# A recurrence feeding a mixture layer on one core: other numbers in the plan's model of transfers, three weight tiles in halves, and the first loads in halves under a limit of bytes in flight

## The chip, the cores and the metric

The kernel runs on one core of a Trainium2 chip. The metric is the device time of one execution in microseconds, as the median of several executions. The profile shows one execution in detail; its own time stands beside the median below.

## The reference

Two layers follow one another. The first is a linear recurrence for 4 batches and 8 heads with 48 dimensions and 768 steps; a state of 48 x 48 is decayed by a sigmoid of a gate, takes in the product of k and v, and is read by q. The second takes the 3072 tokens of 384 features through a layer with 2048 hidden features and the activation mish.

```python
f = 1.0 / (1.0 + np.exp(-f_logit))
for t in range(S):
    state = f[:, :, t, :, None] * state + np.einsum('bhd,bhe->bhde', k[:, :, t], v[:, :, t])
    y[:, :, t] = np.einsum('bhd,bhde->bhe', q[:, :, t], state)
...
h = x @ w_in
sp = np.where(h > 20.0, h, np.log1p(np.exp(np.minimum(h, 20.0))))
g = h * np.tanh(sp)
return (g @ w_out).astype(np.float32)
```

## The kernel before

**Work.** The recurrence is done in 24 chunks of 128 steps (6 blocks of time x 4 batches), numbered so that four chunks in a row, one of each batch, make a group of 512 tokens. A chunk's attention (`prep`, `attn0` to `attn3`) takes two loads of 0.524 MB, one with gates and k (`lk`) and one with q and v (`qv`); it ends with the attended columns in `xt`, or, for the first group, in `xs`. The second layer runs over 6 groups (g) and 16 tiles of 128 hidden features (j): nine products from `xt` into a bank `h` (`moe_in`, line 227), mish on ScalarE and VectorE (`mish`, lines 243 to 258), nine products into three banks `o` (`moe_out`, line 265). Values are split into a high and a low part, so that three products stand for one. For the first group the first four tiles (`WHOLE = 4`) are multiplied unsplit instead (`whole_in`, line 235, and `whole_out`, line 238).

**Weights.** Both weight matrices come as 64-bit data, 0.786 MB per tile j, into one of two `raw` buffers. `load_w` loads a tile and unpacks it with one operation of ScalarE and three of VectorE, of which line 371 is the last and frees the raw buffer; `split_w` makes the high and low part.

**Order.** Every step is added to a `Plan` with its engine, an estimated cost, the step that issues it, and what it reads and writes. The plan then packs all steps onto the engines, forwards and backwards in turn and under several settings, ranks them by how late each may run, and keeps the order whose modelled end is earliest. It issues the steps in that order, so the order on every engine, and on SP's queue for the loads, is fixed by the plan. In its model a load occupies SP for 500 ns, moves at 0.38 KB per ns behind the loads before it, and its readers may start 1550 ns after (`LATENCY["sp"]`, line 53, and lines 114 and 123). Where the plan sees TensorE idle before the first `whole_out` or `moe_out` step, it issues fillers (`idle`, line 353): products with zeros into a bank that is not in use.

**Halves.** The list `units` (line 652) gives the order of (g, j, columns) in the second layer. Tile 0 of the first group is worked in two halves of 256 columns (`EARLY_J = 1`), chunks 0 and 1 first, then 2 and 3; all others have 512 columns. A unit's products out come two units after its products in (`LAG = 2`). The units share two banks `h`, two buffers of mish and three of its result, by the unit's number. `EARLY = 24` says for which units mish squares on ScalarE and takes the low part on VectorE; later ones square on VectorE and take the low part on GpSimd. `attend_goal` says how many attention steps are added before each unit.

**Pacing.** `fetch` (line 342) issues a load on SP's queue. Loads 3 to 11 wait until the load three before them has landed (`AHEAD`, `PACED`); later ones wait only until their buffer is free.

Of the kernel before, what the change touches and what calls it, by code (L numbers as in the profile page):

```python
# [11 lines left out]
I32 = mybir.dt.int32  # L12
# [7 lines left out]
P = 128  # L20
C = 128
CH = C // 2
# [14 lines left out]
LAG = 2  # L37
L_CAP = -40.0
NTRI = GC
PACED = 12  # L40
AHEAD = 3
EARLY = 24
EARLY_J = 1
WHOLE = 4


class Plan:
# [2 lines left out]

    LATENCY = {"pe": 230.0, "act": 170.0, "dve": 160.0, "pool": 180.0, "sp": 1550.0}
    FREE = {"pe": 1500.0, "act": 1900.0, "dve": 1200.0, "pool": 2100.0, "sp": 600.0}

    def __init__(self):
# [3 lines left out]
    def add(self, engine, cost, issue, reads=(), writes=(), size=0, port=False):  # L60

        n = len(self.steps)
        before = {self.writer[r] for r in reads if r in self.writer}
        for w in writes:
            before |= set(self.readers.get(w, ()))
            before |= {self.writer[w]} if w in self.writer else set()
        for r in reads:
            self.readers.setdefault(r, []).append(n)
        for w in writes:
            self.writer[w], self.readers[w] = n, []  # L70
        before.discard(n)
        self.steps.append((engine, cost, issue, before, size, port or engine == "pool"))

    def pack(self, rank, ahead, haste, back=False):


        steps = self.steps
        count = len(steps)
        engine, cost, port = [s[0] for s in steps], [s[1] for s in steps], [s[5] for s in steps]
        before = [s[3] for s in steps]  # L80
        after = [[] for _ in steps]
        for i in range(count):
            for b in before[i]:
                after[b].append(i)
        if back:
            before, after = after, before
        free = dict.fromkeys(self.FREE, 0.0) if back else dict(self.FREE)
        queue = {e: [] for e in free}
        left, ready, start = [len(b) for b in before], [0.0] * count, [0.0] * count
        for i in range(count):  # L90
            if not left[i]:
                queue[engine[i]].append(i)
        transfers = shared = 0.0
        for _ in range(count):
            best = None
            for e, q in queue.items():
                if q:
                    at = [(max(ready[i], shared) if port[i] else ready[i], i) for i in q]
                    t0 = max(free[e], min(at)[0])
                    _, t, i = min(  # L100
                        (rank[i] + haste * max(0.0, r - t0), max(free[e], r), i)
                        for r, i in at if r <= t0 + ahead
                    )
                    if best is None or t < best[0]:
                        best = t, i
            t, i = best
            e = engine[i]
            queue[e].remove(i)
            start[i] = t
            end = free[e] = t + cost[i]  # L110
            if port[i]:
                shared = end
            if e == "sp" and not back:
                transfers = max(transfers, end + 650.0) + steps[i][4] / 0.38
                end = transfers - 650.0
            for a in after[i]:
                f = a if back else i
                if engine[i] == engine[a] == "pe":
                    lag = 0.0
                else:  # L120
                    lag = self.LATENCY[engine[f]]
                    if back and engine[f] == "sp":
                        lag += steps[f][4] / 0.38
                ready[a] = max(ready[a], end + lag)
                left[a] -= 1
                if not left[a]:
                    queue[engine[a]].append(a)
        return start
# [36 lines left out]
def T_ACT(n, psum=False, bias=0):  # L165
    return n / 1.2 + (50 if psum else 92) + 93 * bias + 2


def T_DVE(n):
    return n / 0.96 + 70  # L170
# [7 lines left out]
def recurrence_moe_kernel(  # L178
# [12 lines left out]
    nc = tc.nc  # L191
# [76 lines left out]
    with tc.tile_pool(name="work", bufs=1) as pool, tc.tile_pool(  # L268
# [28 lines left out]
        def inputs(n):  # L297

            whole, place = (held[n], n) if n in held else (in_[n % 2], n % 2)
            keys = [pairs((x, place)) for x in "lkq"] + [[("v", place)]]  # L300
            return keys, [whole[:, x].rearrange("p (a c) -> p a c", a=NP) for x in range(3)] + [whole[:, 3]], whole

        plan = Plan()
        add = plan.add
# [34 lines left out]

        issued = []  # L340

        def fetch(dst, src):

            ins = nc.sync.dma_start(dst, src)
            if AHEAD <= len(issued) < PACED:
                tc.add_manual_dep(
                    ins.ins, issued[-AHEAD].ins.name,
                    mybir.DependencyInfo(mybir.DependencyClass.Sync, mybir.DependencyReason.SCHED_ONLY), reason="pace",
                )
            issued.append(ins)  # L350

        def idle():
            nc.tensor.matmul(zeros[:, 0:P], state0[:, 0:P], state0[:, 0:P], start=True, stop=True)
# [2 lines left out]
        def load_w(j):  # L356

            raw, t = raw_[j % 2], wt_[j % 2]  # L360
            low, high = raw[:, :, 0], raw[:, :, 1]
            kr, kt = ("raw", j % 2), ("wt", j % 2)
            whole, kw = (first[j].bitcast(I32), ("first", j)) if j < HF else (t, kt)
            add("sp", 500, lambda: fetch(raw.rearrange("p a b -> p (a b)"), ww[j].bitcast(I32)),
                (), [kr], 786)
            add("act", T_ACT(W_TILE), lambda: nc.scalar.activation(
                t.bitcast(F32), high.bitcast(F32), AF.Copy, scale=2.0**-112), [kr], [kt])
            add("dve", 480, lambda: nc.vector.tensor_scalar(t, t, 3, None, ALU.logical_shift_left), (), [kt], port=True)
            add("dve", T_DVE(W_TILE), lambda: nc.vector.scalar_tensor_tensor(  # L369
                t, low, 29, t, ALU.logical_shift_right, ALU.bitwise_or), [kr], [kt], port=True)  # L370
            add("dve", T_DVE(W_TILE), lambda: nc.vector.scalar_tensor_tensor(
                whole, high, -(2**31), t, ALU.bitwise_and, ALU.bitwise_or), [kr, kt], [kw], port=True)

        def split_w(j):
            w, kw = (first[j], ("first", j)) if j < HF else (wt_[j % 2].bitcast(F32), ("wt", j % 2))
            old = [[], []]
            if j >= HF:
                old = [
                    [k for n in held for x in inputs(n)[0] for k in x]
                    + [("s", ("xt", 0, c), t) for c in range(GC) for t in range(NP)],  # L380
                    [("first", i) for i in range(HF)],
                ]
            add("act", T_ACT(W_TILE), lambda: nc.scalar.activation(weights(j)[0], w, AF.Copy), [kw], [("w", "h", j)] + old[0])
            add("dve", T_DVE(W_TILE), lambda: nc.vector.tensor_tensor(
                weights(j)[1], w, weights(j)[0].bitcast(F32), ALU.subtract), [kw, ("w", "h", j)],
                [("w", "l", j)] + old[1], port=True)
# [10 lines left out]
        def load(n):  # L397
            keys, _, whole = inputs(n)
            for x, src in ((0, lk), (2, qv)):
                add("sp", 500, lambda x=x, src=src: fetch(whole[:, x : x + 2], src[n]),  # L400
                    (), keys[x] + keys[x + 1], 524)

        def prep(n, parts):
# [237 lines left out]
        steps = [(f, n) for n in range(GC + 1) for f in (start, attn1, attn2, attn3)][:-1]  # L641
# [9 lines left out]

        units = [(0, j, x) for x in range(2) for j in range(EARLY_J)] + [(0, j, 2) for j in range(EARLY_J, HF)]
        units += [(1, j, 2) for j in range(HF)] + [(g, j, 2) for g in range(2) for j in range(HF, NF)]
# [3 lines left out]
        def attend_goal(u):  # L657

            per = 4 * GC
            u = u // 2 if u < 2 * EARLY_J else u - EARLY_J  # L660
            if u < NF + HF:
# [61 lines left out]
        for u in range(len(units) + LAG):  # L723
            if u < len(units):
                g, j, part = units[u]
                whole = g == 0 and j < WHOLE
                if g == 0 and part != 1:
                    load_w(j)
                    if not whole:
                        split_w(j)  # L730
                if u == EARLY_J + WHOLE:
                    split_x()
                if g == 1 and j < WHOLE:
                    split_w(j)
                x, hs, us, gs = g % 2, u % 2, u % 2, u % 3
# [32 lines left out]
    with tc.If(good < total):  # L768
# [3 lines left out]
        with tc.tile_pool(name="slow", bufs=1) as pool, tc.tile_pool(  # L772
# [9 lines left out]
            with tc.For_i(0, B, 1) as b:  # L782
                with tc.For_i(0, NP, 1) as p:
                    f, k, q = (st([P, NCB, C], nm) for nm in ("sf", "sk", "sq"))
# [34 lines left out]
            with tc.For_i(0, NG, 1) as g:  # L819
                x = st([P, NK, GT], "sx")  # L820
                tok = ds(g * GT, GT)
                rows = xs.rearrange("(a e r m) t -> a e m r t", e=2, r=D // 3, m=3)
                with tc.For_i(0, NK, 1) as a:
                    for e in range(2):
                        for m in range(4):
                            src = rows[ds(a, 1), e, m, :, tok] if m < 3 else rows[NP - 1, e, ds(a, 1), :, tok]
# [7 lines left out]
                n, g_ = (st([P, GT], nm) for nm in ("sn", "sg"))  # L834
# [89 lines left out]
```

## Time and profile before

| What | Value |
|---|---|
| Median of 3 runs | 511.36 us (509.66 to 512.45) |
| Profiled execution: its own time | 512.86 us |
| Profiled execution: span from first to last instruction | 511.1 us |
| TensorE busy | 492.9 us, 96% |
| ScalarE busy | 357.9 us, 70% |
| VectorE busy | 340.6 us, 67% |
| GpSimd busy | 143.8 us, 28% |
| Mean granted TensorE clock | 0.99 |
| Loads and stores on SP's queue | 47.59 MB |

The shares are means over the whole span; the fillers count as TensorE's work in them. The work before about 60 us (loads, the first chunks, the first weights) differs from the long steady part behind it, so the rows below are taken by stretch. An idle time "<-issue" is one for which the profile shows nothing that was waited for.

### The profile page before, as it was taken

The numbers are of one execution on the slowest core, as the hardware profiler recorded it, in microseconds if no ns is written. First come the engines' busy times: TensorE is split into PE (matmuls) and PEld (weight loads), VectorE is DVE, ScalarE is ACT, GpSimd is POOL, SyncE is SP. The second block draws the span as 40 slices with busy tenths as digits, with TensorE's granted clock in tenths as the row PEclk, the third lists the DMA queues.
The fourth block names the chain that finished last, engine by engine and source line by source line (L and its number), as shares of the span: only waits on it lengthen the run. The fifth ranks groups of instructions, "written<-read, shape, count | busy, mean of one in ns | idle before, by whom it ended". The sixth has DMA issues, their size and how long they took to land.

```text
span 511.1 us, 12735 instructions
## 1 busy us (share of the span) xinstructions
PE 492.9 (96%) x5320; PEld 391.9 (77%) x5320; DVE 340.6 (67%) x584; ACT 357.9 (70%) x675; POOL 143.8 (28%) x126
## 2 busy tenths in 40 slices
PE   7789999989999999999999999999999999999994
PEld 7676567868788777787888788788788878888883
DVE  4598999989955775877577676586676454534441
ACT  6488998889986676676676676676686655655560
POOL 0331111100002343253343344244252223332421
PEclk9799999999999999999999999999999999999998
DMA  8855664444300542511121221121130000010001
GB/s 283 294 170 206 206 201 166 166 146 162 113 12 0 165 140 105 179 49 42 58 100 42 107 81 42 42 94 63 58 122 9 3 3 31 22 41 1 0 0 68
DMA packets 14800, 48.45 MB, mean 95 GB/s; under 512 B 1744, under 2 KB 1744, under 8 KB 14736
## 3 DMA queue, kind: packets, MB, share of 16 engines
q1 hardware_dynamic: 14736, 47.59, 26.8%
q8 instruction: 42, 0.69, 0.5%
q14 instruction: 22, 0.18, 0.1%
HBM read 39.32 MB, written 6.29 MB: 89 GB/s over the span
## 4 chain that ended last, share of the span: by engine, by line
PE 82%; DMA 6%; DVE 5%; ACT 2%; issue 2%; SPq 0%; DVEq 0%; ACTq 0%
PE o L265 35%; PE h L227 34%; DMA raw<-ww 3%; DMA in<-lk 2%; PE at L564 2%; PE at L552 2%; PE at L509 2%; PE at L468 2%; PE o L238 1%; PE at L576 1%; DMA spareh<-lk 1%; DMA in<-qv 1%; PE h L235 1%; DVE inv L430 1%; DVE wt L369 1%
## 5 line engine op out<-in xcount | busy, mean ns | idle before, releaser
L227 PE MATMUL h<-xt,wh 128*128 128x512 f32 x552 | 173.4, 395 | 2.3 <-DVE ng L256 1.6
L248 POOL TENSOR_TENSOR gl<-ng,gh 128x512 fp32r<-128x512 f32 x73 | 101.7, 1395 | 246.8 <-ACT gh L258 166.8
L227 PEld LDWEIGHTS h<-xt,wh 128*128 128x128 f32 x552 | 102.4, 188 | 26.7 <-DVE ng L256 3.7
L265 PE MATMUL o<-gh,wh 128*128 128x512 f32 x276 | 111.0, 402 | 0.0
L265 PE MATMUL o<-gl,wh 128*128 128x512 f32 x276 | 108.1, 392 | 0.0
L227 PE MATMUL h<-xt,wl 128*128 128x512 f32 x276 | 108.0, 391 | 0.0
L265 PE MATMUL o<-gh,wl 128*128 128x512 f32 x276 | 107.7, 390 | 0.0
L254 ACT ACTIVATE ng<-ng,half 128x512 f32<-128x512 f32 (+1 forms) x97 | 69.6, 717 | 48.5 <-DVE ng L244 46.5
L256 DVE SCALAR_TENSOR_TENSOR ng<-ng,h 128x512 f32<-128x512 f32 x92 | 63.1, 685 | 55.3 <-ACT ng L255 54.3
L252 DVE TENSOR_SCALAR ng<-ng 128x512 f32<-128x512 f32 (+1 forms) x97 | 47.7, 492 | 64.2 <-ACT ng L251 63.8
L251 ACT ACTIVATE ng<-h 128x512 f32<-128x512 f32 (+1 forms) x97 | 57.1, 589 | 43.8 <-PE h L227 43.3
L258 ACT ACTIVATE gh<-ng 128x512 fp32r<-128x512 f32 x92 | 57.5, 625 | 14.3 <-DVE ng L256 10.9
L255 ACT ACTIVATE ng<-ng 128x512 f32<-128x512 f32 (+1 forms) x97 | 60.4, 622 | 1.5
L265 PEld LDWEIGHTS o<-gh,wh 128*128 128x128 f32 x276 | 51.8, 188 | 12.0
L227 PEld LDWEIGHTS h<-xt,wl 128*128 128x128 f32 x276 | 51.8, 188 | 11.9
L265 PEld LDWEIGHTS o<-gl,wh 128*128 128x128 f32 x276 | 51.8, 188 | 11.8
L265 PEld LDWEIGHTS o<-gh,wl 128*128 128x128 f32 x276 | 51.9, 188 | 10.5
L244 DVE TENSOR_TENSOR ng<-ng 128x512 f32<-128x512 f32 x73 | 53.7, 736 | 2.2
L310 POOL TENSOR_TENSOR in<-in,inv 128x512 f32<-128x512 f32 x20 | 24.3, 1217 | 71.1 <-ACT inv L436 46.4
L430 DVE TENSOR_TENSOR_SCAN inv<-gate,state 128x516 f32<-128x516 f32 x20 | 24.9, 1243 | 1.6 <-ACT gate L421 1.4
L598 POOL TENSOR_TENSOR state<-tmp,ends 128x192 f32<-128x192 f32 x20 | 13.7, 682 | 26.1 <-PE at L552 15.7
L624 DVE TENSOR_TENSOR xt<-at,xt 128x256 fp32r<-128x256 f32 x40 | 15.8, 419 | 7.3 <-ACT xt L623 6.9
(135 smaller groups left out, 528.8 us busy)
## 6 DMA issues: line engine op xcount, KB each, us to landing
raw<-ww SPq DMA_DIRECT2D x16, 768.0 KB, 4.2
in<-lk SPq DMA_DIRECT2D x22, 512.0 KB, 3.8
in<-qv SPq DMA_DIRECT2D x22, 512.0 KB, 3.6
out<-ob SPq DMA_DIRECT2D x18, 256.0 KB, 2.3
xt<-xt SPq DMA_DIRECT2D x15, 128.0 KB, 2.5
half<-ob SPq DMA_DIRECT2D x6, 256.0 KB, 2.3
ob<-half SPq DMA_DIRECT2D x6, 256.0 KB, 3.2
spareh<-lk SPq DMA_DIRECT2D x2, 512.0 KB, 5.2
```

Source lines behind the costliest of these rows:

```text
L227: nc.tensor.matmul(h, w[:, a * P : (a + 1) * P], xt[:, x, a, cols], start=(n == 0), stop=(n == 3 * NK - 1))
L244: ("dve", T_DVE(w), 1, lambda: nc.vector.tensor_tensor(n, n, n, ALU.mult))
L248: ("pool", T_POOL(w), 1, lambda: nc.gpsimd.tensor_tensor(gl, g, gh.bitcast(F32), ALU.subtract))
L251: ("act", T_ACT(w, True), 0, lambda: nc.scalar.activation(n, h, AF.Exp)),
L252: ("dve", T_DVE(w / 2), 1, lambda: nc.vector.tensor_scalar(n, n, E_CAP, 1.0, ALU.min, ALU.add)),
L254: ("act", T_ACT(w, False, 1), 0, lambda: nc.scalar.activation(g, n, AF.Ln, bias=half1, scale=0.5)),
L255: ("act", T_ACT(w), 0, lambda: nc.scalar.activation(g, g, AF.Exp, scale=-1.0)),
L256: ("dve", T_DVE(w), 0, lambda: nc.vector.scalar_tensor_tensor(gw if whole else g, g, 1.0, h, ALU.subtract, ALU.mult)),
L258: ("act", T_ACT(w), 0, lambda: nc.scalar.activation(gh, g, AF.Copy)),
L265: nc.tensor.matmul(o, w, x, start=(first and i == 0), stop=(last and i == 2))
L310: add("pool" if on_pool else "dve", cost, lambda: eng.tensor_tensor(dst, x, y, ALU.mult), reads, writes, port=port)
L430: add("dve", 2 * T_DVE(w + st) - 70, lambda s=s, st=st: nc.vector.tensor_tensor_scan(inv1[:, s].rearrange("p a c -> p (a c)"), gate[:, s]. ...
```

## The change

Three things change together. The model of transfers in the plan gets a rate of 0.32 in place of 0.38 KB per ns and a delay of 2400 in place of 1550 ns. `EARLY_J` goes from 1 to 3, so tiles 0, 1 and 2 of the first group are worked in halves of 256 columns: the three first halves, then the three second halves. And each of the first 16 loads is issued as two transfers, of rows 0 to 63 and of rows 64 to 127; each of the 32 waits for the latest earlier one without which at most 1100 KB, itself included, are in flight.

```diff
-PACED = 12
-AHEAD = 3
+PACED = 16
+FLIGHT = 1100
 EARLY = 24
-EARLY_J = 1
+EARLY_J = 3
...
-    LATENCY = {"pe": 230.0, "act": 170.0, "dve": 160.0, "pool": 180.0, "sp": 1550.0}
+    LATENCY = {"pe": 230.0, "act": 170.0, "dve": 160.0, "pool": 180.0, "sp": 2400.0}
...
-                transfers = max(transfers, end + 650.0) + steps[i][4] / 0.38
+                transfers = max(transfers, end + 650.0) + steps[i][4] / 0.32
...
-                        lag += steps[f][4] / 0.38
+                        lag += steps[f][4] / 0.32
...
-        def fetch(dst, src):
-
-            ins = nc.sync.dma_start(dst, src)
-            if AHEAD <= len(issued) < PACED:
-                tc.add_manual_dep(
-                    ins.ins, issued[-AHEAD].ins.name,
-                    mybir.DependencyInfo(mybir.DependencyClass.Sync, mybir.DependencyReason.SCHED_ONLY), reason="pace",
-                )
-            issued.append(ins)
+        def fetch(dst, src, size):
+
+            early = len(issued) < 2 * PACED
+            for r in (slice(0, CH), slice(CH, P)) if early else (slice(0, P),):
+                ins = nc.sync.dma_start(dst[r], src[r])
+                if early:
+                    issued.append((ins, size / 2))
+                    flight, n = 0, len(issued)
+                    while n and flight + issued[n - 1][1] <= FLIGHT:
+                        n -= 1
+                        flight += issued[n][1]
+                    if n:
+                        tc.add_manual_dep(
+                            ins.ins, issued[n - 1][0].ins.name,
+                            mybir.DependencyInfo(mybir.DependencyClass.Sync, mybir.DependencyReason.SCHED_ONLY), reason="pace",
+                        )
```

The two callers of `fetch` pass the size of the load, 786 for weights and 524 for a chunk.

## Rows read from the trace of the kernel before

**Rows 1.** Stretches: length, busy PE, PEld, DVE, ACT, POOL; clock, DMA share, GB/s.

```profile
6.50:16.00 9.50, 9.10 (x202) 7.76 (x203) 4.32 (x11) 8.65 (x23) 2.29 (x2) 1.00 0.93 319
16.00:19.40 3.40, 0.03 (x3) 0.00 (x0) 1.02 (x2) 0.98 (x2) 0.71 (x2) 0.99 0.93 351
19.40:26.20 6.80, 6.79 (x96) 6.03 (x99) 5.10 (x8) 2.46 (x6) 1.58 (x2) 0.50 0.74 242
26.20:41.00 14.80, 12.99 (x401) 11.02 (x393) 13.91 (x21) 13.08 (x33) 4.36 (x4) 1.00 0.48 171
41.00:57.50 16.50, 15.37 (x194) 8.97 (x190) 14.93 (x30) 14.71 (x31) 2.87 (x3) 1.00 0.63 211
57.50:110.00 52.50, 50.23 (x700) 36.85 (x700) 49.88 (x83) 45.60 (x87) 7.22 (x7) 1.00 0.54 184
...
135.00:160.00 25.00, 25.00 (x110) 20.13 (x109) 16.66 (x28) 20.76 (x36) 1.13 (x1) 1.00 0.13 43
160.00:504.50 344.50, 344.17 (x3514) 276.78 (x3512) 207.80 (x357) 224.47 (x417) 122.53 (x98) 1.00 0.17 59
```

**Rows 2.** The waits of TensorE, 0 to 40 us: total, times, longest.

```profile
PE h L468 <- issue: 3.4, 1, 3.4
```

**Rows 3.** Groups by form, 26.2 to 41 us: total busy us, mean ns.

```profile
L353 PE MATMUL o<-state 128*128 128x128 f32 x16 | 2.4, 281 | 0.0
```

**Rows 4.** Timeline of SP's queue: start us, duration us, issue.

```profile
0.75 0.39 SPq L344 DMA_DIRECT2D in<-lk  x1
...
4.47 1.53 SPq L344 DMA_DIRECT2D spareh<-lk  x2
...
16.72 0.33 SPq L344 DMA_DIRECT2D in<-lk  x1
19.28 0.33 SPq L344 DMA_DIRECT2D in<-qv  x1
```

**Rows 5.** The chain of waits, 40 to 110 us: start us, us, what.

```profile
42.64 6.13 DMA raw<-ww
...
99.31 6.66 DMA raw<-ww
```

**Rows 6.** The waits of ScalarE, 0 to 140 us.

```profile
ACT wt L366 <- DMA raw<-ww: 4.0, 3, 2.0
```

**Rows 7.** The waits of TensorE, 40 to 130 us.

```profile
PE h L227 <- DVE ng L256: 1.6, 1, 1.6
```

**Rows 8.** Timeline of VectorE: the unpacking of weight tiles 1 and 2 ends.

```profile
28.78 0.94 DVE L371 SCALAR_TENSOR_TENSOR sparel<-raw,wt 128x768 int32<-128x768 int32 x1
...
36.62 1.71 DVE L371 SCALAR_TENSOR_TENSOR sparel<-raw,wt 128x768 int32<-128x768 int32 x1
```

**Rows 9.** Timeline of TensorE, 20 to 54 us.

```profile
21.28 1.13 PE L468 MATMUL o<-spareh 48*64 48x64 f32 x32
...
31.91 1.46 PE L235 MATMUL h<-spareh,sparel 128*128 128x256 f32 x6
...
40.98 1.56 PE L235 MATMUL h<-spareh,sparel 128*128 128x256 f32 x6
...
52.75 1.56 PE L238 MATMUL o<-ob,sparel 128*128 128x256 f32 x6
```

**Rows 10.** Groups by form, 30 to 60 us: mish at 512 and 256 columns.

```profile
L251 ACT ACTIVATE ng<-h 128x512 f32<-128x512 f32 x3 | 1.8, 587 | 0.0
...
L254 ACT ACTIVATE ng<-ng,half 128x512 f32<-128x512 f32 x2 | 1.4, 722 | 0.0
...
L254 ACT ACTIVATE ng<-ng,half 128x256 f32<-128x256 f32 x2 | 1.0, 506 | 0.0
...
L251 ACT ACTIVATE ng<-h 128x256 f32<-128x256 f32 x2 | 0.8, 384 | 0.0
```

**Rows 11.** The page: costliest groups; DMA issues, us to landing.

```profile
L244 DVE TENSOR_TENSOR ng<-ng 128x512 f32<-128x512 f32 x73 | 53.7, 736 | 2.2
...
raw<-ww SPq DMA_DIRECT2D x16, 768.0 KB, 4.2
```

More of the change, by code (lines that the diff above doesn't have):

```diff
@@ L363, in load_w @@
             whole, kw = (first[j].bitcast(I32), ("first", j)) if j < HF else (t, kt)
-            add("sp", 500, lambda: fetch(raw.rearrange("p a b -> p (a b)"), ww[j].bitcast(I32)),
+            add("sp", 500, lambda: fetch(raw.rearrange("p a b -> p (a b)"), ww[j].bitcast(I32), 786),
                 (), [kr], 786)
@@ L399, in load @@
             for x, src in ((0, lk), (2, qv)):
-                add("sp", 500, lambda x=x, src=src: fetch(whole[:, x : x + 2], src[n]),
+                add("sp", 500, lambda x=x, src=src: fetch(whole[:, x : x + 2], src[n], 524),
                     (), keys[x] + keys[x + 1], 524)
```

## The prediction

> **What bounds the kernel now.** I read four views in this order. First the stages, as busy time in stretches [rows 1]. From 57.5 us on TensorE is full: 50.23 of 52.50 us up to 110 us, 25.00 of 25.00 between 135 and 160, 344.17 of 344.50 up to 504.5 us. Only 2.27 us are lost in the first of these and 0.33 in the last. So whatever the change brings must come out of the first 57.5 us, or out of those 2.27. VectorE and ScalarE stand beside it at 49.88 and 45.60 of 52.50 us between 57.5 and 110 us, and VectorE falls to 16.66 of 25 us after 135 us: early on the engines that unpack weights are nearly full too.
>
> Second, where the early time of TensorE goes. The profile calls an engine busy that runs the fillers of line 353 (products with zeros, into a bank that nobody reads yet), so the busy column flatters. [...] Between 26.2 and 41.0 us TensorE is busy 12.99 of 14.80 us [rows 1], and 2.4 us of that is fillers [rows 3]: 1.8 + 2.4 = 4.2 us without useful work. From 41.0 to 57.5 us 1.13 us are idle [rows 1].
>
> Third, the transfers. SP issues the early loads in order; the third-latest must have landed before the next is issued. Read so, the issue at 4.47 us is the landing of the first load (0.524 MB), and that at 19.28 us the landing of the ninth, the second weight tile [rows 4]. By then seven loads of 0.524 MB and two of 0.786 MB have landed, 5.24 MB, so the stream runs at (5.24 - 0.52) / (19.28 - 4.47) = 0.319 MB per us. The first load took 4.47 - 0.75 = 3.7 us. The old plan believed 0.38 and 0.50 + 1.38 + 1.55 = 3.4 us; the new one 0.32 and 0.50 + 1.64 + 2.40 = 4.5 us. For the rate the new number is what the trace shows. At 0.38 the 5.24 MB are over 2.6 us earlier than at 0.32, so the old plan placed consumers too early.
>
> Fourth, what that error costs behind 41 us: the chain of waits has the raw weight loads of 42.64 and 99.31 us, 6.13 and 6.66 us long [rows 5], where the old model gives 0.50 + 2.07 + 1.55 = 4.1 us and the new one 0.50 + 2.46 + 2.40 = 5.4. ScalarE stood 4.0 us in front of raw weights in the first 140 us [rows 6]. TensorE felt it as 1.6 us in front of a product after mish [rows 7].
>
> **The change part by part.** All sums are made against the profiled execution, 512.86 us (a span of 511.1 us). The median of the runs shown is 511.36 us, 1.5 us below, and I subtract the same gap from it.
>
> **Three tiles in halves (EARLY_J, line 43; units, line 652).** The first product of a tile can start when chunks 0 and 1 have been attended, not all four. Before, only tile 0 did. Now tiles 1 and 2 may too. Tile 1's unpacking ends at 28.78 + 0.94 = 29.7 us [rows 8]; its half can lie in the 4.2 us hole between 26 and 41 us. A half costs 1.46 us in and 1.56 us out [rows 9], 3.0 us. I credit 2.5 us: bounds are 0 (it only displaces other work) and 4.2 (the whole hole). Tile 2 is unpacked at 36.62 + 1.71 = 38.3 us [rows 8], too late for the hole; its half gains nothing. It may even cost: the units share two h banks, two mish buffers and the o banks in the order of the list, and tile 2's first half now stands ahead of the second halves of 0 and 1. Tile 0's second half ran at 40.98 us [rows 9], 2.7 us after 38.3, so as long as tile 2 is no more than some 2 us later than before nothing waits for it. The price: two tiles run mish twice at 256 columns. Two of ScalarE's four operations show the extra, 2 x 0.384 - 0.587 = 0.18 us and 2 x 0.506 - 0.722 = 0.29 us [rows 10]; eight operations at 0.235 make 1.9 us of ScalarE, which is 14.71 of 16.50 us busy between 41.0 and 57.5 us [rows 1], so some 0.8 us will show (bounds 0 and 1.9). Two late tiles of group 0 also change form, because EARLY counts units: their subtraction goes to GpSimd and their square to VectorE, which has 8.3 of 25 us free there [rows 1]. That costs nothing under this cover, and 2 x 0.736 = 1.5 us without it [rows 11].
>
> **The plan's model (lines 53, 114 and 123).** Consumers of a load are placed later and loads earlier, on all queues. The gain is bounded by TensorE's waits that go back to a late load: 1.13 us between 41.0 and 57.5 us and 1.6 of the 2.27 behind, 2.8 us in all [rows 1, 7]; below by 0, or by a loss of the same size if the new order puts something else late. For a raw tile on its own the new model is too slow (median 4.2 us to landing against its 5.4) [rows 11], so some consumers stand later than they need. I take 2.2 us. More delay in the plan also means more fillers before the first product; they lie in front of the first data and cost nothing.
>
> **Halves of 64 rows and 1.1 MB in flight (line 342 on).** The first 16 loads become 32 issues. SP pays an issue of 0.33 us [rows 4] for 16 more, 5.3 us on a queue that waits for landings most of that time; each consumer waits for two landings in place of one. In flight were three loads, 1.57 MB or more; now four halves of 0.262 MB, or two of 0.393 with one of 0.262. A load of 0.524 MB took 3.7 us, of which 1.6 us at 0.32 is the moving, so 2.1 us is delay; a window of 1.05 MB turns over in 2.1 + 0.8 = 2.9 us, 0.36 MB per us, just above the rate of the stream. Two weight halves alone, 0.786 MB in 3.3 us, give 0.24, so a weight tile beside another costs up to 0.9 us. I take 0.6 us for bubbles (bounds 0 and, with a lower rate, rival 2). Nothing lands earlier by it, since the loads were already in order.
>
> **Sum:** -2.5 - 2.2 + 0.8 + 0.6 = -3.3 us: 509.5 us for the profiled execution, **508.0 us** for the median. Its own range, from the bounds of the two credits, is 505 to 511 us.
>
> **Rivals.** (1) *The gain is taken by the unpacking.* TensorE gets ahead, but between 57.5 and 110 us VectorE has only 52.50 - 49.88 = 2.6 us free [rows 1], and TensorE, 3 us earlier, waits there for mish and weights. For it: those digits. Against it: part of VectorE's work there unpacks weights used long after. That gives 510.8 us (509.5 to 514).
>
> (2) *Slower: the halves move at a lower rate.* Each transfer now writes 64 neighbouring rows, and all in flight sit on SP's one queue, one behind another. No row shows such a transfer; a load of 128 rows is the nearest, at 0.319 MB per us. If halves run at two thirds, 0.21, the ninth load (5.24 MB) lands at some 2 + 25 = 27 us instead of 19.3, and tile 1 is unpacked 8 us later, at the end of the hole: the 2.5 us are gone. The eighth load, q and v of chunk 2 (4.46 MB, landed when the issue of 16.72 us goes out [rows 4]), lands at 23 us, and TensorE, which took its scores at 21.28 us [rows 9], would stand some 4 us later, 2.5 us of which the hole behind takes back. Net 4 - 2.5 + 0.8 + 0.6 = +2.9 us on the median, 514.3 us (511.5 to 518). It decides below about 4.46 / (21.3 - 2 - 3) = 0.27 MB per us, with 3 us from landing to the scores; above that nothing on the path is late. [...]
>
> (3) *Faster: the stall at 16 us and the slow clock go.* The 3.4 us are no wait for data that the trace shows, and the new plan has other fillers and another order in front of that place. If the stall falls on a gap, 3.4 us and half of the 6.8 us at 0.50 [rows 1, 2] are saved, less what the chunk loads would hold up then: some -4.5 us more than the forecast, 503.5 us (500 to 506). As easily it stays or falls elsewhere.
>
> **How the numbers follow.** Forecast 0.42, rival 1 0.20, rival 2 0.26, rival 3 0.12. A difference under 0.5% (2.6 us: under 508.8 is faster, over 513.9 slower) is about what a measurement can't tell from none. Of the forecast 0.30 lies under 508.8 and 0.12 between; of rival 1 0.18 between and 0.02 above; of rival 2 0.05 between and 0.21 above; rival 3 is faster. Faster 0.42, same 0.35, slower 0.23. The range for 8 in 10 leaves out most of rival 3 below and the upper part of rival 2: 502.5 to 516.5 us.
>
> **What would show it.** Right: products of line 235 at 256 columns for three tiles, tile 1's first before 41 us, and fewer fillers after 26 us; TensorE full from about 54 us; raw weights no longer waited for by ScalarE. Rival 1: new waits of TensorE for mish or the low part of weights between 55 and 110 us. Rival 2: well under the 319 GB/s of before between 6.5 and 16 us [rows 1], with the DMA share still high. Rival 3: no stretch at 0.50. The prediction is wrong if TensorE's useful work at 57.5 us is not ahead of before by about 3 us.

## The result, and the profile after

| Kernel | Median of 4 runs | Against before, 95% interval | Profiled execution |
|---|---|---|---|
| before | 511.14 us | 1 | 512.86 us |
| changed | 516.42 us | 1.0107 (1.0069 to 1.0146) | 515.46 us |

The changed kernel is slower by 1.1%, 5.3 us of the medians. The forecast was 508.0 us and faster; the time is inside the range, close to its upper end, on the side of rival 2. The profiled executions differ by only 2.6 us: the one of after is its fastest, the one of before is slower than each of the runs that make its median.

The stretches of the changed kernel, with the columns of [rows 1]: length, busy time of the engines, granted clock, DMA share, GB/s.

```profile
core 0: us, PE busy (x) PEld busy (x) DVE busy (x) ACT busy (x) POOL busy (x), PEclk, DMA share, GB/s
6.50:16.00 9.50, 7.85 (x141) 6.98 (x140) 3.63 (x10) 7.33 (x20) 0.00 (x0) 1.00 0.96 229
16.00:19.40 3.40, 1.84 (x50) 1.45 (x42) 0.00 (x0) 2.48 (x6) 2.96 (x3) 1.00 0.76 184
19.40:26.20 6.80, 4.60 (x80) 4.18 (x80) 4.50 (x8) 2.74 (x8) 0.11 (x1) 0.55 0.87 216
26.20:41.00 14.80, 11.17 (x287) 9.37 (x286) 9.29 (x17) 8.00 (x19) 2.37 (x3) 0.86 0.77 191
41.00:57.50 16.50, 13.50 (x270) 11.22 (x269) 11.58 (x24) 13.27 (x35) 3.40 (x4) 1.00 0.67 193
57.50:110.00 52.50, 51.77 (x772) 38.85 (x771) 52.18 (x94) 49.72 (x98) 10.34 (x8) 1.00 0.62 211
...
160.00:507.00 347.00, 347.00 (x3529) 279.49 (x3528) 208.32 (x363) 225.67 (x424) 125.02 (x99) 1.00 0.17 59
```

Against [rows 1]: the DMA engines are as busy between 6.5 and 16 us (0.96, before 0.93), but they move 229 GB/s where they moved 319. TensorE falls behind in every stretch up to 57.5 us but that of 16.0 to 19.4, where the "issue" stall of before lay, 3.4 us [rows 2]. Up to 57.5 us its busy time is 7.85 + 1.84 + 4.60 + 11.17 + 13.50 = 39.0 us; before it was 9.10 + 0.03 + 6.79 + 12.99 + 15.37 = 44.3. These sums count the fillers, whose groups between 6.5 and 57.5 us are, before and changed:

```profile
L353 PE MATMUL o<-state 128*128 128x128 f32 x28 | 3.9, 279 | 0.0
...
L360 PE MATMUL o<-state 128*128 128x128 f32 x31 | 4.8, 286 | 0.0
```

Without them TensorE did 34.2 us of useful work there and 40.4 before. It is 6.2 us behind, not 3 ahead, which is the prediction's own sign of being wrong. Behind 57.5 us the kernel is better than before: 51.77 of 52.50 us busy against 50.23, and 347.00 of 347.00 at the end.

The chain of waits of the first 60 us: first the shares by line, then start, duration, what.

```profile
by line: DMA in<-qv 30.1%; DMA raw<-ww 24.3%; DMA spareh<-lk 7.4%; SPq L346 4.9%; PE at L432 3.3%; ACT wt L373 2.9%; ACT xt L399 2.6%; ACT ng L254 2.2%; PE h L475 1.9%; PE at L516 1.8%; issue 1.7%; ACT ng L243 1.5%; ACT ng L255 1.5%; PE at 
...
0.75 0.61 SPq L346
...
2.67 4.91 DMA in<-qv
...
17.23 3.50 DMA in<-qv
...
21.60 1.13 PE h L475 x32
...
27.56 0.62 PE o L475 x32
```

Loads make up most of it almost from the start: q/v and weight loads are 54% of it. The scores of chunk 1 (bank h, line 475 of the changed kernel) run at 21.60 us, right behind a q/v load that landed at 20.7; those of chunk 2 (bank o) run at 27.56 us, where before they ran at 21.28 [rows 9]. SP's own issuing is 4.9% of 60 us, 2.9 us.

The waits of TensorE up to 60 us, and of ScalarE up to 140 us: total, times, longest.

```profile
PE h L475 <- DVE in L310: 2.9, 1, 2.9
PE at L617 <- ACT spareh L612: 2.7, 1, 2.7
```

```profile
ACT wt L373 <- DMA raw<-ww: 5.7, 5, 2.8
```

ScalarE stands longer in front of raw weights than before (5.7 us, before 4.0 [rows 6]), though the plan now expects later landings. VectorE finishes the unpacking of tiles 1 and 2:

```profile
36.57 0.95 DVE L378 SCALAR_TENSOR_TENSOR sparel<-raw,wt 128x768 int32<-128x768 int32 x1
...
47.31 0.95 DVE L378 SCALAR_TENSOR_TENSOR sparel<-raw,wt 128x768 int32<-128x768 int32 x1
```

That is 37.5 us for tile 1, where it was 29.7, and 48.3 for tile 2, where it was 38.3 [rows 8]. And the first four halves, from the timeline of TensorE (one line is one half of one tile):

```profile
32.79 1.46 PE L235 MATMUL h<-spareh,sparel 128*128 128x256 f32 x6
...
37.58 2.93 PE L235 MATMUL h<-spareh,sparel 128*128 128x256 f32 x6 [0.64 <-DVE sparel L378]
...
48.82 1.56 PE L235 MATMUL h<-spareh,sparel 128*128 128x256 f32 x6
...
51.64 1.46 PE L235 MATMUL h<-spareh,sparel 128*128 128x256 f32 x6
```

Tile 1's first half did run before 41 us, as forecast, at 37.58 us, right behind the unpacking of its weights. The third line is the first half of tile 2, at 48.82 us, again right behind its weights. The second half of tile 0 stands behind it in the list and came at 51.64 us, where before it ran at 40.98 [rows 9].

### The profile page after: what moved, and what is told of

Read it like the earlier page. It is cut to its first block, busy times and chain, and to the rows that moved or that the text cites. A ratio compares the mean times of both kernels' runs of the same rounds, so it can differ in the third digit from the quotient of the medians.

```text
span 513.7 us, 12829 instructions
## 1 busy us (share of the span) xinstructions
PE 493.8 (96%) x5352; PEld 398.0 (77%) x5352; DVE 333.2 (65%) x588; ACT 356.8 (69%) x681; POOL 147.1 (29%) x128
## 4 chain that ended last, share of the span: by engine, by line
PE 80%; DMA 8%; ACT 5%; DVE 4%; issue 1%; SPq 1%; DVEq 0%; ACTq 0%
PE o L265 36%; PE h L227 35%; DMA raw<-ww 4%; DMA in<-qv 4%; PE at L559 2%; PE at L571 2%; PE at L516 2%; PE at L475 1%; PE at L583 1%; DMA spareh<-lk 1%; ACT wt L373 1%; DVE wl L391 1%; SPq L346 1%; ACT wh L390 1%; DVE gl L247 0%
## 5 line engine op out<-in xcount | busy, mean ns | idle before, releaser
L248 POOL TENSOR_TENSOR gl<-ng,gh 128x512 fp32r<-128x512 f32 x75 | 104.9, 1401 | 250.1 <-ACT gh L258 156.1
L252 DVE TENSOR_SCALAR ng<-ng 128x512 f32<-128x512 f32 (+1 forms) x99 | 49.5, 500 | 57.4 <-ACT ng L251 56.6
L437 DVE TENSOR_TENSOR_SCAN inv<-gate,state 128x516 f32<-128x516 f32 x20 | 27.5, 1374 | 7.4 <-ACT gate L428 7.4
```

Source lines behind the costliest of these rows:

```text
L248: ("pool", T_POOL(w), 1, lambda: nc.gpsimd.tensor_tensor(gl, g, gh.bitcast(F32), ALU.subtract))
L252: ("dve", T_DVE(w / 2), 1, lambda: nc.vector.tensor_scalar(n, n, E_CAP, 1.0, ALU.min, ALU.add)),
L437: add("dve", 2 * T_DVE(w + st) - 70, lambda s=s, st=st: nc.vector.tensor_tensor_scan(inv1[:, s].rearrange("p a c -> p (a c)"), gate[:, s]. ...
```

## The experiments

The theories: R, a transfer of 64 neighbouring rows is slow; S, one of 64 rows is, whichever they are; P, the new order of the plan is the cost; W, the limit of bytes in flight is the cost; N, it is the number of transfers. Each ratio is against runs of the kernel before that were taken beside that run, so medians of different runs are not compared directly. Where the text says "the changed kernel with", the edit shown is against the changed kernel, and so it is for the halves alone; the other edits are against the kernel before.

### The change taken apart

The halves alone: the new `fetch` in the kernel before, with its order.

```diff
-EARLY_J = 3
+EARLY_J = 1
-... "sp": 2400.0}
+... "sp": 1550.0}
-... steps[i][4] / 0.32
+... steps[i][4] / 0.38
```

> The kernel before with one part of the change alone: the first 16 loads as two transfers of rows 0 to 63 and 64 to 127 under the limit of 1100 KB. The order on every engine is that of before. Theory R (64 neighbouring rows move slower; after showed 229 GB/s against 319 between 6.5 and 16 us at the same DMA share): the rate falls to about 0.24 MB per us here too, the ninth load lands some 6 us later, and the time is 514 to 519 us against 511. Theory P (the new order of the plan is the cost, the rate matters little): 510 to 512 us. Theory W (the limit on bytes in flight starves the queue, not the rows): slower as well, 513 to 518 us, but with a DMA share well under 0.9 between 6.5 and 16 us.

Measured: 521.04 us, 1.0194 (1.0150 to 1.0238). Two stretches of it, and ScalarE's wait up to 140 us:

```profile
6.50:16.00 9.50, 7.00 (x96) 6.09 (x96) 3.37 (x9) 6.21 (x17) 0.00 (x0) 0.82 1.02 227
...
41.00:57.50 16.50, 12.25 (x165) 10.48 (x166) 9.40 (x17) 11.81 (x27) 3.15 (x3) 0.69 0.57 154
```

```profile
ACT wt L373 <- DMA raw<-ww: 13.6, 5, 5.0
```

227 GB/s at a share of 1.02 (the share adds up the times of all packets, and here they come to more than the 16 engines' time): theory R, and W is out, since the engines are full. The loss is larger than that of the whole change, and than the 514 to 519 us that I expected. ScalarE stands 13.6 us in front of raw weights, 4.0 before [rows 6], and TensorE does only 12.25 us of work between 41 and 57.5 us, at a clock of 0.69. Its scores of chunk 2 and its second half of tile 0:

```profile
24.20 1.13 PE L475 MATMUL o<-spareh 48*64 48x64 f32 x32 [3.56 <-DVE spareh L310]
...
54.24 1.56 PE L235 MATMUL h<-spareh,sparel 128*128 128x256 f32 x6
```

The scores are 2.9 us later than before, the half 13.3 us [rows 9], with the order of before: most of the delay arises behind the scores.

The plan and the tiles without the halves: the constants of after, `fetch` of before.

```diff
-EARLY_J = 1
+EARLY_J = 3
-... "sp": 1550.0}
+... "sp": 2400.0}
-... / 0.38
+... / 0.32
```

> The change without its transfers: the plan's new rate and delay and the three tiles in halves, but whole loads of 128 rows, paced three apart as before. The order on every engine is that of after. Theory R: 319 GB/s between 6.5 and 16 us as before, and the gain that was forecast for these two parts, 2.5 + 2.2 - 0.8 us, so some 507 to 510 us. Theory P: about 516 us as after, since the order is the same.

Measured: 508.28 us, 0.9955 (0.9926 to 0.9983). Two of its stretches, ScalarE's wait up to 140 us, and two waits of TensorE up to 60 us:

```profile
6.50:16.00 9.50, 8.94 (x178) 7.77 (x179) 3.84 (x11) 8.11 (x21) 1.99 (x3) 1.00 0.96 331
...
57.50:110.00 52.50, 51.73 (x717) 39.84 (x716) 51.92 (x89) 48.97 (x92) 9.60 (x7) 1.00 0.61 203
```

```profile
ACT wt L366 <- DMA raw<-ww: 0.8, 1, 0.8
```

```profile
PE o L564 <- issue: 3.3, 1, 3.3
PE o L468 <- issue: 1.9, 1, 1.9
```

331 GB/s, and ScalarE waits 0.8 us for raw weights. With the same order the halves cost 1.0107 / 0.9955 = 1.015, some 8 us; theory P falls, since the order here is that of after. TensorE gains 1.5 us between 57.5 and 110 us (51.73, before 50.23 [rows 1]). Its "issue" stall is still there, now 3.3 and 1.9 us.

The plan's numbers alone.

```diff
-... "sp": 1550.0}
+... "sp": 2400.0}
-... / 0.38
+... / 0.32
```

> The kernel before with the plan's rate of 0.32 and delay of 2400 ns alone; whole loads, one tile in halves. Theory R with my forecast for this part: 2.2 us faster, 508 to 511 us, and ScalarE's waits for raw weights under 2 us in the first 140 us in place of 4.0. If the order is what costs (theory P) and it comes from the model: 513 to 517 us.

Measured: 509.46 us, 0.9966 (0.9944 to 0.9989): 1.7 us, with an interval from 0.6 to 2.9. Two of its stretches, and a wait of TensorE between 40 and 130 us:

```profile
41.00:57.50 16.50, 16.50 (x254) 9.92 (x253) 16.16 (x31) 15.59 (x33) 2.41 (x3) 1.00 0.58 193
57.50:110.00 52.50, 49.51 (x645) 35.24 (x647) 50.06 (x83) 45.41 (x86) 7.79 (x7) 1.00 0.51 174
```

```profile
PE h L227 <- DVE ng L256: 1.5, 1, 1.5
```

The profile shows no wait of ScalarE for raw weights in the first 140 us, and no idle time of TensorE between 41 and 57.5 us. But the wait for mish is 1.5 us, as good as before (1.6 [rows 7]), and between 57.5 and 110 us TensorE is busy 49.51 us, not more than before (50.23 [rows 1]). The execution in this profile is the slowest of the twelve, 512.55 us, so it doesn't show where the 1.7 us come from.

The three tiles alone.

```diff
-EARLY_J = 1
+EARLY_J = 3
```

> The kernel before with three tiles in halves alone; old model of transfers, whole loads. My forecast for this part was 2.5 us won and 0.8 us paid: 508 to 511 us, with the first half of tile 1 before 41 us. If tile 2's late weights hold the units behind it, 511 to 514 us.

Measured: 510.98 us, 1.000 (0.9977 to 1.0024): nothing, within 1.2 us. The timeline of TensorE:

```profile
31.93 2.07 PE L235 MATMUL h<-spareh,sparel 128*128 128x256 f32 x6
...
34.44 1.56 PE L235 MATMUL h<-spareh,sparel 128*128 128x256 f32 x6
...
38.25 1.56 PE L235 MATMUL h<-spareh,sparel 128*128 128x256 f32 x6
...
43.23 1.46 PE L235 MATMUL h<-spareh,sparel 128*128 128x256 f32 x6
```

All three first halves ran before 41 us, and the second half of tile 0 came at 43.23 us, 2.2 us later than before [rows 9]. The hole was filled with work that had been done a little later anyway.

### Which property of the halves is slow

Even and odd rows in place of the first and the last 64.

```diff
-            for r in (slice(0, CH), slice(CH, P)) if early else (slice(0, P),):
+            for r in (slice(0, P, 2), slice(1, P, 2)) if early else (slice(0, P),):
```

> The changed kernel with one edit: a half load is the even rows or the odd rows, not the first or the last 64. Sizes, number of transfers, limit in flight and order on every engine are those of after. Theory R in its narrow form (it is the neighbourhood of the rows that costs): the rate returns to 0.30 to 0.33 MB per us and the time to that of the plan and tiles with whole loads, 508 to 512 us. Theory W (limit in flight) or a cost per transfer: the rate stays at about 0.24 and the time at 516 us.

Measured: 520.51 us, 1.0192 (1.0150 to 1.0234), slower than after, which no theory had. Two of its stretches, and a wait of TensorE:

```profile
2.00:6.00 4.00, 4.00 (x22) 4.00 (x20) 1.58 (x11) 0.63 (x3) 0.00 (x0) 1.00 0.87 282
...
16.00:19.40 3.40, 0.00 (x0) 0.00 (x0) 0.00 (x0) 0.00 (x0) 0.00 (x0) 0.50 0.83 240
```

```profile
PE at L516 <- DMA in<-lk: 15.9, 1, 15.9
```

The rate is nearer to that of whole loads: 282 GB/s at a share of 0.87 between 2 and 6 us, 324 while the engines move, where the changed kernel has this row there, 255 while moving:

```profile
2.00:6.00 4.00, 4.00 (x21) 4.00 (x20) 1.32 (x10) 0.24 (x2) 0.00 (x0) 1.00 0.96 245
```

But the time tells nothing of the rate: between 16.0 and 19.4 us all engines stand still, and TensorE waits 15.9 us at line 516, the product of k and v of chunk 0, for a load of gates and k that it doesn't read. That wait is new with the strided rows; where it comes from I didn't settle. The packets tell more. The trace has the size and the time of every packet, the piece in which a transfer is moved; those of a chunk's load are of 4096 bytes. Between 6.5 and 16 us the median packet of 4096 bytes takes 159 ns with even and odd rows, 159 in the kernel before and 282 in the changed kernel. So half of the rows, interleaved, move packet by packet as fast as whole loads do.

Halves by columns, of all 128 rows, with the same number and size of transfers.

```diff
-            for r in (slice(0, CH), slice(CH, P)) if early else (slice(0, P),):
-                ins = nc.sync.dma_start(dst[r], src[r])
+            pieces = [((x, x[:, :1], x[:, 1:]) if len(x.shape) == 3 else (x, x[:, : W_TILE], x[:, W_TILE :])) for x in (dst, src)]
+            for d, s in zip(*(z[1:] if early else z[:1] for z in pieces)):
+                ins = nc.sync.dma_start(d, s)
```

> The changed kernel with one edit: a half load is half of the columns of all 128 rows (for a chunk the one or the other of its two arrays), not 64 of the rows. Number and size of the transfers, the limit of 1100 KB and the order on every engine are those of after; a row's piece is 2 to 3 KB in place of 4 to 6. Theory R (few rows per transfer is the cost): 0.31 MB per us or more in the first 16 us and 507 to 511 us, as with whole loads. Theory N (the number of transfers or the limit is the cost): about 0.24 MB per us and 515 to 517 us.

Measured: 509.13 us, 0.9960 (0.9930 to 0.9990). Its stretch from 6.5 to 16 us:

```profile
6.50:16.00 9.50, 8.94 (x179) 7.73 (x178) 3.82 (x10) 7.75 (x20) 2.53 (x3) 1.00 0.83 264
```

Theory N falls: 32 transfers and the limit, and the loss is gone. 264 GB/s is under the 0.31 MB per us that I expected; at a share of 0.83 it is 318 while moving. The engines are now idle for part of the time, so the limit of 1100 KB begins to show. ScalarE's wait for raw weights up to 140 us:

```profile
ACT wt L375 <- DMA raw<-ww: 8.2, 4, 4.8
```

It is longer than in the changed kernel (5.7 us), and the time is 1.5% better: this wait alone does not set the time.

Halves of 64 rows with twice the limit.

```diff
-FLIGHT = 1100
+FLIGHT = 2200
```

> The changed kernel with the limit at 2200 KB in place of 1100; halves of 64 rows as in after. Theory R: the DMA engines were already full (share 0.96 between 6.5 and 16 us), so the rate stays at 0.23 to 0.25 MB per us and the time at 514 to 518 us. Theory W (the limit starves the queue): the rate returns to 0.32 and the time to 508 to 510 us.

Measured: 516.97 us, 1.0100 (1.0068 to 1.0133). The same stretch:

```profile
6.50:16.00 9.50, 8.35 (x108) 7.82 (x108) 3.72 (x10) 6.76 (x18) 0.00 (x0) 0.82 1.04 234
```

The share is 1.04 and the rate 234 GB/s: twice the limit didn't help these transfers.

The rates by themselves, before all other work: four groups of extra loads, each started when the one before has landed.

```diff
+            for t, rows in (
+                (low, [slice(0, 64)] * 4),
+                (mixed, [slice(32, 96)] * 4),
+                (None, [slice(0, 128)] * 2),
+                (turns, [slice(0, 64), slice(64, 128)] * 2),
+            ):
...
+                    ins = nc.sync.dma_start(dst[r], src[r])
...
             plan.issue()
```

> The kernel before with four groups of extra loads in front of everything, each of 1.05 MB into memory that is unused then, each group started when the one before has landed: four transfers of rows 0 to 63; four of rows 32 to 95; two of rows 0 to 127; and rows 0 to 63 and 64 to 127 by turns, four. Only the rates of the groups are of interest; the time is some 25 us longer. [...]

One run, 531.9 us. The stretches in which each group moves (rows 0 to 63; rows 32 to 95, and one microsecond inside it; all rows; the turns):

```profile
2.00:6.70 4.70, 3.27 (x16) 2.97 (x14) 1.02 (x9) 0.54 (x3) 0.00 (x0) 1.00 0.98 220
9.20:13.30 4.10, 0.00 (x0) 0.00 (x0) 0.00 (x0) 0.00 (x0) 0.00 (x0) 1.00 0.81 252
10.00:11.00 1.00, 0.00 (x0) 0.00 (x0) 0.00 (x0) 0.00 (x0) 0.00 (x0) 1.00 1.00 397
15.20:18.30 3.10, 0.00 (x0) 0.00 (x0) 0.00 (x0) 0.00 (x0) 0.00 (x0) 1.00 0.87 320
20.20:24.90 4.70, 0.00 (x0) 0.00 (x0) 0.00 (x0) 0.00 (x0) 0.00 (x0) 1.00 1.00 241
```

Rows 0 to 63 move at 220 GB/s at a share of 0.98. By turns with 64 to 127 it is 241 at 1.00, but 241 x 4.7 us are 1.13 MB, and the group has 1.05: the rest is of the kernel's own first loads, and the group alone moves at some 223. Rows 32 to 95, as many and as neighbouring, reach 397 GB/s at a share of 1.00 for one microsecond; over the group it is 252 at 0.81, with gaps that I can't explain. All 128 rows, ends of the stretch included, move at 320 at 0.87. The rate of the group of rows 32 to 95 would not settle it, but its packets do: the median packet of 4096 bytes takes 311 ns for rows 0 to 63, 284 by turns, 159 for rows 32 to 95 and 159 for all rows. So theory S falls, and R holds only for neighbours on one side of row 64: slow here are the transfers that stay in one half of the rows, 311 and 284 ns a packet against 159.

By turns, transfers of rows 0 to 63 and of rows 64 to 127 are in flight together (the four are issued between 18.87 and 21.28 us), and their 223 GB/s can't be told from the 220 of rows 0 to 63 alone. Rows 0 to 63 against all 128 are 220 against 320, a ratio of 0.69. Why a transfer within one half of the rows is the slower one, no run shows.

### The limit

Whole loads with the limit of 1100 KB.

```diff
-            early = len(issued) < 2 * PACED
-            for r in (slice(0, CH), slice(CH, P)) if early else (slice(0, P),):
+            early = len(issued) < PACED
+            for r in (slice(0, P),):
...
-                    issued.append((ins, size / 2))
+                    issued.append((ins, size))
```

> The changed kernel with whole loads of 128 rows and the limit of 1100 KB kept for the first 16: two chunk loads in flight, a weight tile alone beside at most nothing. Theory R: the rate while the engines move is over 0.33, but the DMA share falls to 0.6 to 0.8 because the limit is coarser, so the mean between 6.5 and 16 us is 0.22 to 0.28 MB per us; 509 to 515 us. If the limit alone explained the loss of after, 516 us or more.

Measured: 515.59 us, 1.0075 (1.0054 to 1.0097). The same stretch:

```profile
6.50:16.00 9.50, 8.79 (x174) 7.62 (x174) 3.73 (x10) 7.98 (x20) 1.47 (x2) 1.00 0.67 226
```

226 GB/s at a share of 0.67, so 337 while moving: the same mean rate as in the changed kernel, for the other reason, and nearly the same loss, just over the 509 to 515 us that I expected. In whole loads this limit leaves the engines idle for a third of the stretch; the weight tiles go alone.

Halves by columns, as above, with 1600 and with 2200 KB, and whole loads with 2200. The edit of the first; the others have 2200 there:

```diff
-FLIGHT = 1100
+FLIGHT = 1600
```

> The changed kernel with halves by columns of all 128 rows and a limit of 1600 KB. With 1100 KB the DMA share was 0.83 between 6.5 and 16 us at 264 GB/s. If that share was the limit at work, it rises to 0.9 or more and the rate to 0.30 MB per us; the time is 505 to 509 us, no worse than whole loads three apart (508.3). If the limit keeps something else short, 509 to 511 us.

> As the one before with 2200 KB: share over 0.93 and 0.31 to 0.33 MB per us between 6.5 and 16 us; 505 to 509 us. If a limit is worth something by itself (less in front of a needed transfer), it is slower than with 1600 KB by up to 2 us; the loads are in order either way, so I expect no difference.

> The changed kernel with whole loads of 128 rows and a limit of 2200 KB: four chunk loads in flight, or two weight tiles and one chunk. The order on every engine is that of after. If halves by columns are worth something in themselves (an array that is ready while the other still moves), this is slower than they are at the same limit: 507 to 510 us against 505.4. If only rate and depth matter, 504 to 507 us.

Measured: 506.48 us, 0.9905 (0.9875 to 0.9934); 505.38 us, 0.9883 (0.9853 to 0.9912); whole loads 506.58 us, 0.9922 (0.9890 to 0.9955). All three beat both kernels. The stretch from 6.5 to 16 us, by columns with 1600 KB, by columns with 2200 and in whole loads with 2200:

```profile
6.50:16.00 9.50, 8.97 (x179) 7.74 (x177) 3.83 (x11) 8.41 (x21) 2.55 (x3) 1.00 0.96 330
6.50:16.00 9.50, 8.94 (x178) 7.78 (x177) 3.72 (x11) 7.72 (x20) 1.87 (x3) 1.00 1.04 383
6.50:16.00 9.50, 8.94 (x179) 7.78 (x179) 3.87 (x11) 8.11 (x21) 2.02 (x3) 1.00 0.91 326
```

A later stretch of the 2200 KB by columns, and ScalarE's wait for raw weights:

```profile
26.20:41.00 14.80, 14.80 (x260) 12.35 (x261) 11.95 (x21) 11.77 (x29) 2.00 (x2) 0.88 0.34 108
```

```profile
ACT wt L375 <- DMA raw<-ww: 0.6, 1, 0.6
```

The rate rises with the limit, 264, 330 and 383 GB/s for 1100, 1600 and 2200 KB of column halves, and so does the share, 0.83, 0.96 and 1.04; 383 is above the 310 to 330 that I expected. The time follows: 1100 and 2200 KB are apart beyond their intervals, 1600 and 2200 are not. Whole loads at 2200 KB move 326 GB/s, no faster than in the run with plan and tiles (331), and their time can't be told from that of column halves at 2200, nor from that run. So the rate of this stretch alone does not order the times. By columns with 2200 KB TensorE is busy without a gap from 26.2 to 41 us, fillers included, and ScalarE waits 0.6 us for raw weights.

## Why the prediction was wrong

**The transfers.** The step that failed is "I take 0.6 us for bubbles": it priced the halves at the rate of a whole load. Measured with the order held fixed, the halves cost some 8 us in the order of after (1.0107 against 0.9955) and 9.9 us (0.0194 of 510) in that of before. The window was a smaller error. By my sum 1.05 MB in flight feed 0.36 MB per us, and column halves under the same limit moved only 0.264, but they cost no time beyond the plan and tiles (0.9960 against 0.9955).

Rival 2 named the cause and the boundary: below 0.27 MB per us the path is late, and the rate was 0.23 to 0.245. Its range, 511.5 to 518 us, holds the measured time; its sum was too small, +2.9 us against the measured +5.3. Its two thirds, 0.21 MB per us, came from no row; between 6.5 and 16 us the changed kernel moved 0.229, 0.72 of the 0.319 of before. It had tile 1 unpacked 8 us later, and it was, at 37.5 us in place of 29.7. It priced chunk 2's scores as 4 us late, and they were 27.56 - 21.28 = 6.3 us late. What it did not count is what happens behind these places. The prediction held that nothing waits for tile 2's first half if that is no more than some 2 us later than before; its weights were unpacked 9.9 us later, and tile 0's second half ran behind it, 10.7 us later than before. Tile 2 is not the whole of it: with the halves alone, where only tile 0 is in halves, that half was 13.3 us late. How the loss divides among these places stays open. The granted clock is at most a part: its mean between 19.4 and 41 us is 0.76 in the changed kernel and 0.84 before [rows 1], but it is 0.76 too with whole loads and 2200 KB, which beat both kernels.

And with no row for such a transfer I took the rate of the nearest one as the likelier, and gave the rival a chance of 0.26; a term that no row shows and that the whole early stream hangs on deserved at least even odds.

**The plan's model.** Forecast 2.2 us won, measured 1.7 (0.6 to 2.9): the size was right. Half of the mechanism was: with the plan's numbers alone ScalarE no longer waits for raw weights, and the 1.13 us of idle time between 41 and 57.5 us are gone. The other half was not: the 1.6 us in front of a product after mish were put down to late weights, and they are still 1.5 us in the run where ScalarE waits for no weights. TensorE won its 1.5 us between 57.5 and 110 us only with the tiles in halves as well. One thing was not forecast: the new model may be a protection. The same slow halves cost the old order 1.9% and the new one 1.5%, and ScalarE stood 13.6 us in front of raw weights in the one and 5.7 in the other; but the two costs are not apart beyond their intervals.

**Three tiles in halves.** Forecast 2.5 us won and 0.8 paid, measured nothing (1.2 us either way). The halves did move into the hole, as forecast, but the units behind them came later in turn (with the tiles alone, tile 0's second half by 2.2 us). The lower bound of that credit, "it only displaces other work", was the right end.

**The sum without the transfers.** -2.5 - 2.2 + 0.8 = -3.9 us was forecast, -2.3 (-0.9 to -3.8) measured.

**Rival 1** was half seen: VectorE is 51.92 of 52.50 us busy between 57.5 and 110 us in the run with plan and tiles, and TensorE still gained there. **Rival 3** didn't come: the "issue" stall moved, it is 3.3 and 1.9 us in that run, and the slow clock came at another place (a mean of 0.77 between 26.2 and 41 us, where before it was 0.50 from 19.4 to 26.2 us [rows 1]). In the changed kernel the longest waits of TensorE up to 60 us are for other engines and not "issue", and the clock was slow all the same, 0.55 and 0.86 in the two stretches from 19.4 to 41 us.

## What to carry to other kernels

Split a transfer by its columns rather than at row 64: here the split at row 64 cost about 30% of the rate (229 GB/s against 319, and 220 against 320), and twice the limit in flight didn't win it back (234). Parts that have rows on both sides of row 64 moved as fast as whole loads by their packets too (159 ns), but even and odd rows brought a wait of 15.9 us with them, and that kernel was the slower for it. Look at the DMA share beside the GB/s: the same 226 to 229 GB/s was full engines in one kernel (0.96) and a starved queue in another (0.67), with opposite cures. Change the model of a planner together with the transfers it models only when each has been timed alone: here a gain of 0.45% and a loss of 1.5% came as one number.

## What the runs showed of the hardware that I had not expected

The early stream can move more than the 319 GB/s that I took for its rate: 383 GB/s between 6.5 and 16 us with column halves and 2200 KB. The pacing is a part of that, since column halves went from 264 to 383 as the limit rose. It is not all, since whole loads with 2200 KB moved 326; why columns do better there stays open. An issue on SP's queue cost more for halves of 64 rows than the 0.33 us that I took: the first takes 0.61 us in the chain of after, where the first whole load took 0.39 [rows 4], and that chain has 2.9 us of issuing in the first 60 us.
